# Issuing the first image pair's four lines alternately from SyncE and ScalarE, with the projection weight moved behind them

## The chip, the cores and the metric

One core of a Trainium2 chip runs the program. The metric is the device time of one execution in microseconds; most executions of one kernel here fall within about 2 us of each other (0.2%). The kernel before takes 1033.91 us (median), so two per cent, the threshold for "faster" or "slower", is 20.7 us.

## The reference, cut to what matters

```python
# q: 4 x 12288 x 128, kv: 4 x 384 x 32 x 128, w_sr: 128 x 128, all float32
kv_pool = kv.reshape(B, H // 4, 4, W // 4, 4, C).mean(axis=(2, 4))
k = v = kv_pool.reshape(B, -1, C) @ w_sr          # 768 keys a batch
a = softmax(q @ k.T / sqrt(C)); x = a @ v          # attention
out = (relu(x @ w_gate) * (x @ w_val)) @ w_out     # gated feed-forward, d_ff 1536
```

The keys need 4 x 4 pixels of the image averaged and projected by `w_sr`. Nothing can be scored before the first 256 keys exist.

## The kernel before

The image of a batch is loaded in three "pairs" (of key chunks); each pair is four "lines" (`dh` = 0 to 3) of 128 x 1024 floats, 512 KB a line. In the opening (batch 0) TensorE sums the pixels by accumulating transposes in PSUM: eight transposes a line. Then come a copy, the projection by `w_sr`, the scores, the exponentials and the values. Eight filler matmuls ahead of it are to bring TensorE to its full rate.

```python
    def kv_load(b, pair):
        parts = work.tile([128, r, 2, r, C], FP32, tag="kv_in", bufs=3)
        rows = kv[b, ...].rearrange("(hp dh) (wp h dw) c -> dh hp wp (h dw c)", ...)
        for dh in range(r):                       # one DMA a line, all from SyncE
            nc.sync.dma_start(parts[:, dh].rearrange("p h dw c -> p (h dw c)"), rows[dh])
    ...
    w_sr_f32 = const.tile([128, C], FP32)
    nc.scalar.dma_start(w_sr_f32, w_sr)
    kv_load(0, 0)
    for i in range(0, GRP, 2):
        q_load_plain(i, i + 2)                    # two loads of q, SyncE
    for pair in range(1, NJC // 2):
        kv_load(0, pair)                          # eight more lines, SyncE
    ...
    fill(8)
    ...
    for dh in range(3):                           # TensorE takes the lines in order
        for h in range(2):
            turn_add(h, line(0, dh, h), first=dh == 0)
    for h in range(2):
        turn_end(h, line(0, 3, h), (nc.vector, nc.scalar)[h])
    for h in range(2):
        project_chunk(h, (nc.vector, nc.scalar)[h])
    ...                                           # q casts, scores, exponentials, values
    # GpSimd waits for line 2 of the third pair, then loads the feed-forward weights
    nc.gpsimd.tensor_copy(gate, line(2, 2)[:, 0, 0, 0:1])
```

From about 31 us on a long body of fixed order runs, bound by TensorE.

The softmax here doesn't subtract the row's maximum and nothing guards it: scores larger than these inputs give would overflow.

## Time and profile before

| | kernel before |
|---|---|
| median time | 1033.91 us |
| span of the profiled execution | 1031.3 us |
| TensorE's share of the chain that ended last | 98% |
| landing of the four lines | 5.2, 6.5, 8.5, 9.75 us |
| projection of the first pair starts | 10.83 us |
| body starts (first feed-forward matmul) | 30.30 us |

How to read it: a shift of a few tenths of a microsecond in the opening can't be seen in shares of a 1031 us span. It is read from the time at which the same instruction starts in two traces. I use two such marks, the start of the first projection and the start of the body. Landing times here are the last of the 16 completions that a transfer leaves in the trace. I take each completion for that of one of the core's 16 DMA engines; the trace doesn't name the engine. The single completions come from the trace's own list, which no view prints.

### The profile page before, as it was taken

Reading aid. Unit: us, or ns where it says so; the run is one execution under the profiler, and the core shown is the slowest. Engines: PE = TensorE matmul, PEld = TensorE weight load, DVE = VectorE, ACT = ScalarE, POOL = GpSimd, SP = SyncE. Lnnn points to the kernel's source line nnn. Section 1 sums busy time; section 2 is a strip of 40 time slices with the busy share of each in tenths; the row PEclk is TensorE's granted clock in tenths of the full one; section 3 lists DMA queues with packets and bytes.
Section 4 is the critical chain, followed back from the end, with each engine's and each line's share of the span. In section 5 each row is a group of like instructions: output and inputs, shape, how many; then the busy total and the mean of one; then the engine's idle time right before and its main releaser. Section 6 shows DMA issues by size and latency. Waiting matters only on the chain.

```text
span 1031.3 us, 20032 instructions
## 1 busy us (share of the span) xinstructions
PE 1024.4 (99%) x6580; PEld 546.0 (53%) x6580; DVE 910.0 (88%) x1671; ACT 908.8 (88%) x1745; POOL 279.4 (27%) x287
## 2 busy tenths in 40 slices
PE   8999999999999999999999999999999999999998
PEld 6555555555555555555555555555555555555555
DVE  3889899998989898998889898989888898989898
ACT  4988888889888889888888898888888988888987
POOL 2212146521211125642212121664121221111110
PEclk9999999999999999999999999999999999999999
DMA  8836396462542547836345157573652434513222
GB/s 305 122 57 76 90 195 144 79 93 42 82 69 48 80 120 162 169 53 90 52 68 86 33 84 151 131 173 57 85 73 46 73 54 65 87 32 65 34 40 54
DMA packets 328824, 93.34 MB, mean 91 GB/s; under 512 B 308496, under 2 KB 321936, under 8 KB 328720
## 3 DMA queue, kind: packets, MB, share of 16 engines
q1 hardware_dynamic: 313488, 78.69, 38.7%
q0 software_dynamic: 14944, 13.24, 10.9%
q8 instruction: 51, 0.84, 0.4%
q14 instruction: 53, 0.43, 0.1%
q10 hardware_dynamic: 288, 0.13, 0.0%
HBM read 53.94 MB, written 26.35 MB: 78 GB/s over the span
## 4 chain that ended last, share of the span: by engine, by line
PE 98%; ACT 1%; DMA 1%; SPq 0%; DVE 0%; issue 0%; ACTq 0%
PE bank_ps L279 24%; PE bank_ps L290 24%; PE bank_ps L314 23%; PE bank_ps L241 13%; PE bank_ps L230 12%; PE bank_ps L300 1%; DMA parts<-in_kv_dram 1%; PE bank_ps L163 1%; ACT aT L231 0%; PE bank_ps L189 0%; PE bank_ps L181 0%; SPq L139 0%; ACT val L283 0%; ACT kv L183 0%; PE bank_ps L119 0%
## 5 line engine op out<-in xcount | busy, mean ns | idle before, releaser
L293 DVE SCALAR_TENSOR_TENSOR hT<-bank_ps,val 128x512 f16<-128x512 f32 x1152 | 757.9, 686 | 91.1 <-ACT val L283 70.5
L283 ACT CAST val<-bank_ps 128x512 f16<-128x512 f32 x1152 | 677.8, 589 | 102.5 <-PE bank_ps L279 100.5
L279 PE MATMUL bank_ps<-xT,wv 128*128 128x512 f16 x1152 | 436.6, 379 | 0.2 <-DVE rinv L249 0.2
L290 PE MATMUL bank_ps<-xT,wg 128*128 128x512 f16 x1152 | 436.6, 379 | 0.0
L314 PE MATMUL bank_ps<-hT,wo 128*128 128x512 f16 x1116 | 423.0, 379 | 0.0
L231 ACT ACTIVATE aT<-bank_ps 128x512 f16<-128x512 f32 x576 | 345.8, 604 | 1.0 <-PE bank_ps L230 1.0
L324 POOL TENSOR_SCALAR o_sb<-o_t 128x512 f32<-128x512 f32 x93 | 138.3, 1487 | 694.1 <-DVE rinv L249 660.0
L241 PEld LDWEIGHTS <-aT 128*128 128x128 f16 x2304 | 177.3, 98 | 133.1 <-issue 0.9
L241 PE MATMUL bank_ps<-kv,aT 128*128 128x129 f16 x2304 | 223.6, 220 | 0.0
L230 PE MATMUL bank_ps<-qT,kv 128*128 128x512 f16 x576 | 217.3, 379 | 0.4 <-DVE qT L122 0.2
L279 PEld LDWEIGHTS <-wv 128*128 128x128 f16 x1152 | 112.7, 98 | 132.7 <-issue 0.3
L290 PEld LDWEIGHTS <-wg 128*128 128x128 f16 x1152 | 112.7, 98 | 67.3
L314 PEld LDWEIGHTS <-wo 128*128 128x128 f16 x1116 | 109.2, 98 | 65.9 <-issue 0.2
L230 PEld LDWEIGHTS <-kv 128*128 128x128 f16 x576 | 56.1, 98 | 67.6 <-issue 0.8
L257 DVE TENSOR_TENSOR x<-bank_ps,rinv 128x256 f16<-128x256 f32 x190 | 80.6, 424 | 6.6
L322 DVE STREAM_TRANSPOSE o_t<-bank_ps 128x512 f32<-128x512 f32 x93 | 65.7, 706 | 0.0
L86 POOL DMA_DIRECT2D q<-in_q_dram x88 | 48.3, 556 | 0.3 <-issue 0.3
L148 POOL TENSOR_TENSOR s<-parts 128x512 f32<-128x512 f32 x36 | 44.8, 1265 | 0.0
L249 DVE RECIPROCAL rinv<-bank_ps 128x2 f32<-128x2 f32 x192 | 27.9, 146 | 0.8 <-PE bank_ps L241 0.8
L150 POOL TENSOR_TENSOR s<-s 128x512 f32<-128x512 f32 x18 | 22.8, 1266 | 1.4
L152 POOL TENSOR_TENSOR c<-s 128x256 f32<-128x256 f32 x18 | 13.0, 724 | 1.4
L300 PEld LDWEIGHTS <-hT 128*128 128x128 f16 x144 | 10.1, 98 | 5.8
(53 smaller groups left out, 94.6 us busy)
## 6 DMA issues: line engine op xcount, KB each, us to landing
parts<-in_kv_dram SPq DMA_DIRECT2D x48, 512.0 KB, 6.5
out_dram<-o_sb SPq DMA_DIRECT2D x353, 64.0 KB, 2.2
q<-in_q_dram POOLq DMA_DIRECT2D x88, 128.0 KB, 4.6
xT<-x SPq DMA_TRANSPOSE x94, 2.4
out_dram<-o_sb SPq DMA_DIRECT2D x80, 16.0 KB, 1.5
placed<-blocks SPq DMA_DIRECT2D x9, 128.0 KB, 1.8
kvT<-placed SPq DMA_DIRECT2D x36, 32.0 KB, 1.9
q<-in_q_dram SPq DMA_DIRECT2D x2, 512.0 KB, 8.0
```

The costliest lines, as they stand in the source:

```text
L86: nc.gpsimd.dma_start(q16[32 * j : 32 * (j + 1)].rearrange("t (i s) c -> t i s c", i=GRP), rows[j])
L230: nc.tensor.matmul(s_ps, kv16[:, k // NST, jc, 0:C], qT_of(k), start=True, stop=True)
L231: nc.scalar.activation(aTs[k][:, jc, :], s_ps, AF.Exp, scale=qk_scale)
L241: nc.tensor.matmul(x_ps[:, i, :], aTs[k][:, jc, s * 128 : (s + 1) * 128], kv16[:, k // NST, jc, C : 2 * C + 1], start=(jc == 0 and i == 0) ...
L257: nc.vector.tensor_tensor(x16s[k][:, 2 * half : 2 * half + 2, :], x_ps[:, :, 0:C], rinv.to_broadcast([128, 2, C]), op=ALU.mult,)
L279: nc.tensor.matmul(va_ps, wv16[:, fb * 128 : (fb + 1) * 128], xTs[k], start=True, stop=True)
L283: nc.scalar.copy(val, va_ps)
L290: nc.tensor.matmul(g_ps, wg16[:, fb * 128 : (fb + 1) * 128], xTs[k], start=True, stop=True)
L293: nc.vector.scalar_tensor_tensor(hTs[k][:, fb, :], g_ps, 0.0, vals.pop((k, fb)), op0=ALU.max, op1=ALU.mult)
L314: nc.tensor.matmul(o_banks[k], wo16[:, fb, :], hTs[k][:, fb, :], start=fb == 0, stop=fb == NFB - 1)
L322: nc.vector.transpose(o_t, o_banks.pop(k))
L324: nc.gpsimd.tensor_scalar(o_sb.rearrange("t j s c -> t s j c"), o_t.rearrange("t (s j c) -> t s j c", s=NS, j=4), 1.0 / X_SCALE**2, None, ...
```

## The change

Its intent is to get the first pair's lines in sooner, by having two engines issue them side by side, and to let the weight, which isn't needed until the projection, go after them.

```diff
-    def kv_load(b, pair):
+    def kv_load(b, pair, queues=(nc.sync,)):
...
-            nc.sync.dma_start(parts[:, dh].rearrange("p h dw c -> p (h dw c)"), rows[dh])
+            queues[dh % len(queues)].dma_start(
+                parts[:, dh].rearrange("p h dw c -> p (h dw c)"), rows[dh]
+            )
...
-    nc.scalar.dma_start(w_sr_f32, w_sr)
-    kv_load(0, 0)
+    kv_load(0, 0, (nc.sync, nc.scalar))
+    nc.sync.dma_start(w_sr_f32, w_sr)
```

The values and scores in TensorE's waits of the opening, which the change's name also mentions, stand in both kernels alike.

## The prediction

> **What bounds the kernel now.** I read the page first, then the chain of waits, the timeline of the opening, the transfers, and the landings.
>
> The page's busy shares and chain give the scale:
>
> ```profile
> span 1031.3 us, 20032 instructions
> PE 1024.4 (99%) x6580; PEld 546.0 (53%) x6580; DVE 910.0 (88%) x1671; ACT 908.8 (88%) x1745; POOL 279.4 (27%) x287
> ...
> PE 98%; ACT 1%; DMA 1%; SPq 0%; DVE 0%; issue 0%; ACTq 0%
> ```
>
> TensorE is 98% of the chain that ended last; the change touches nothing in the body after about 31 us, where its order of work is fixed. So the change can only shift the body earlier or later by whatever the opening gains or loses. The chain of waits in the first 12 us shows the part in question:
>
> ```profile
> 0.73 0.70 SPq L139
> ...
> 2.10 0.60 SPq L139
> 2.71 0.04 issue
> 2.75 7.00 DMA parts<-in_kv_dram
> 9.75 0.04 issue
> 9.79 1.09 PE bank_ps L163 x8
> 10.88 0.86 PE bank_ps L181 x4
> ```
>
> SyncE issues the four lines of the first image pair one after the other (about 0.65 us each). The fourth lands at 2.75 + 7.00 = 9.75 us, and TensorE then needs only its own eight transposes, 1.09 us, before the projection. Read naively, three SyncE issues (0.70, 0.58, 0.60, with gaps 2.0 us) stand on the path and an alternation would save most of half of them. The transfers' rate, by slices of 1 us over the first 40, and TensorE's timeline say otherwise:
>
> ```profile
> GB/s 0 50 142 274 397 377 381 434 414 418 410 418 414 418 410 397 414 418 410 397 377 49 10 111 167 195 155 123 110 145 187 188 179 132 143 222 181 130 1 16
> ...
> 5.23 3.13 PE L163 MATMUL bank_ps<-ident,parts 128*128 128x128 f32 x16
> 8.53 1.09 PE L163 MATMUL bank_ps<-ident,parts 128*128 128x128 f32 x8 [0.17 <-DMA parts<-in_kv_dram]
> 9.79 1.09 PE L163 MATMUL bank_ps<-ident,parts 128*128 128x128 f32 x8 [0.17 <-DMA parts<-in_kv_dram]
> ```
>
> From 4 us to 21 us the transfers run at about 410 GB/s without a gap: a 512 KB line every 1.28 us, while SyncE issues one every 0.65 us. Single issues taken by narrow windows land 4.5, 5.0, 6.4 and 7.0 us after issue, that is at 5.2, 6.5, 8.5 and 9.75 us. So the waiting time of line four is the queue, not its issue. What is lost is the ramp: 142 and 274 GB/s in the third and fourth microseconds.
>
> The durations by tile in narrow windows show a second fact:
>
> ```profile
> L163 PE MATMUL bank_ps<-ident,parts x10: 421/421/476, 5.2 to 7.2; 128*128 128x128 f32 x10
> L163 PE MATMUL bank_ps<-ident,parts x8: 273/273/328, 9.8 to 10.6; 128*128 128x128 f32 x8
> ```
>
> The same transpose takes 421 ns (start to start 213 ns) up to about 7.5 us and 273 ns (start to start 109 ns) afterwards. TensorE is slow until then, although the eight filler matmuls began at 1.71 us and the transposes follow them with no pause. The arrival of lines one by one hides this: the 16 slow transposes of lines one and two are done before line three is there.
>
> **What the Trainium skill says.** "DMA: Bandwidth & Descriptors", section "Issuing engines are not separate DMA queues": transfers started by SyncE, ScalarE or GpSimd run on the same 16 engines and interleave; issuing from several saves only issue time. The trace agrees that issue time is not the limit (0.65 us of issue against 1.28 us of transfer). The same page, "Queues, rings and completion order": each DMA engine takes turns, packet by packet, between the queues that have work. Nothing in this trace has two full hardware queues at once, so it isn't shown yet. "TensorE: Matmul & The Clock Gate", Part 1: the array runs at half rate until an activity window of about 3.4 us, free-running, was busy. The trace agrees with the halving (213 against 109 ns), and the switch came at about 7.5 us, 5.8 us after the fillers began, so one mostly busy window did not do.
>
> **The change, part by part.** The work on every compute engine is the same in number and order; only four issues and the weight's load move.
>
> 1. *Issue.* Lines one and three stay with SyncE, two and four go to ScalarE, w_sr goes to SyncE as its third transfer. All four lines are issued by about 2.1 us instead of 3.35. ScalarE's two issues end there, its table load (1.28 us) and warm-up follow, done by about 3.7 us; its first real work is at 10.92 us. Cost on the path: 0. Gain on the path: 0, as the queue is the limit.
>
> 2. *Transfer of the sum.* Four lines are 2 MB whichever queue. w_sr (64 KB) moved at about 2 us, in the empty ramp; now it goes behind line three in a full queue: 64/512 of 1.28 us = 0.16 us later for what comes after it. Two queues from the start may shorten the ramp. About 0.7 MB is missing in it: (410-142)+(410-274) KB = 0.4 MB in two slices and the rest before, so at most 0.4/0.41 = 1 us is there to be had; I allow 0.3 us (choice). Net: the fourth line lands at about 9.75 - 0.3 + 0.16 = 9.6 us, range 9.0 to 9.9.
>
> 3. *Order of landing.* If the engines take turns, lines one and two share the rate and land together, at about 6.4 us (where line two landed), and three and four together, at about 9.5 us. TensorE takes the lines in order. Line one now comes 1.2 us later and line three 1 us later than before.
>    - *TensorE already at full rate:* 16 transposes remain after 9.5 us: 16 x 0.109 = 1.75 us, to 11.25, where before the last eight ended (by start of the projection, 10.83). Loss 0.4 us. Break-even is a landing at 9.1 us.
>    - *TensorE still slow:* fillers end at 5.31; it idles until 6.4. If the window from about 4.2 to 7.6 (the one that seems to have switched it before) isn't busy enough, the switch comes one window later, near 11. Then lines one and two take 16 x 0.213 = 3.4 us, to 9.8; six more by 11.06; ten at 0.109: 12.15. Loss 1.3 us.
>
> 4. *After that.* From 9.79 us to 31 us the chain is compute (transposes, projection, exponentials), so a loss passes whole to the end. A gain passes only as far as the later pairs' lines allow: by their landing times (issue plus time to landing in narrow windows: 5.14 + 9.7, 5.97 + 10.2 and 6.62 + 10.8, so 14.9, 16.2 and 17.4 us for the second pair's last three) TensorE or VectorE takes them up within 0.15 to 0.4 us, so beyond 0.4 us only what the whole stream gains counts.
>
> Sum: probability 0.45 of +1.3 (slow), 0.35 of +0.4 (fast, together), 0.2 of -0.5 (better ramp). 0.585 + 0.14 - 0.1 = +0.6 us. 1033.9 + 0.6 = **1034.5 us**.
>
> **Rivals.**
> - *Issue was the limit:* the fourth line comes 1.3 us sooner (3.35 to 2.1) and the time falls to about 1032.7. For it: the chain names SyncE for 2 us. Against: 10 us of queue before each later landing, and an unbroken 410 GB/s.
> - *The ramp doubles with two queues:* the stream moves up 0.5 to 0.9 us, all pairs with it, and the time is about 1033.2. For it: packets in the ramp move at a third to two thirds of the rate while the DMA engines show over 80% busy (0.89 and 0.83 in these two slices), so each is waiting on something that a second queue might overlap. Against: the engines may be as slow for both.
> - *Hidden anyway:* losses and gains cancel, 1033.9. For it: before, TensorE idled only 0.2 and 0.2 us by the waits view for lines three and four; but the idle time of the pipelined transposes understates it.
> - *w_sr late:* it would hold the projection. Against: it is ahead of q in SyncE's queue and needed a microsecond after line four. No cost.
>
> **Range and chances.** The outcomes span -1.2 (issue theory) to +1.8 (slow, late landing). I take 1033.2 to 1035.8 for 8 in 10. Two per cent is 20.7 us, longer than the whole stretch to which the change reaches, so "within 2%" is 0.99.
>
> **What the profile after would show.** Right: lines one and two landing within 0.3 us of each other near 6.4 us, three and four near 9.5; transposes of 421 ns still running after 8 us; the projection starting at 11.2 to 12.2 instead of 10.83; the body after 31 us equal in length. Wrong: line one still at about 5.2 us (no taking of turns); the GB/s of the third and fourth slice above 300 (the ramp was the queue's); a projection before 10.5 us. The prediction fails if two queues fill the ramp, or if TensorE switches to full rate early however long it waits.

## The result

The changed kernel took 1033.65 us (median of 5 runs, 1033.19 to 1034.54) beside 1033.91 us of the kernel before. The ratio is 0.9999 with a 95% interval from 0.9984 to 1.0013: the same. (A ratio is the mean time of one kernel's fast runs over that of the other's of the same rounds, so not quite the ratio of the medians.)

The chain of waits of the changed kernel in the first 12 us, start, duration, what:

```profile
1.48 7.49 DMA parts<-in_kv_dram
8.96 0.04 issue
9.01 1.97 PE bank_ps L165 x16
10.97 0.86 PE bank_ps L183 x4
```

The reader is to see two things against the chain of before. The last line that TensorE needs is there at 8.96 instead of 9.75 us, 0.78 us sooner. And 16 transposes stand behind it where eight stood: 1.97 us for 1.09 us. The gain is given back on the spot, and the projection (L183) starts at 10.92 instead of 10.83 us.

TensorE's timeline in the same stretch (start, duration, group, idle before and its cause):

```profile
6.39 1.97 PE L165 MATMUL bank_ps<-ident,parts 128*128 128x128 f32 x16 [1.24 <-DMA parts<-in_kv_dram]
9.01 1.97 PE L165 MATMUL bank_ps<-ident,parts 128*128 128x128 f32 x16 [0.65 <-DMA parts<-in_kv_dram]
```

The lines are taken in two blocks of two, with a wait before each. The transfers in narrow windows of issue time (queue, size, us from issue to landing; the first two lines were issued at 0.73 us by both engines, the other two at 1.41 and 1.48 us) tell why:

```profile
parts<-in_kv_dram ACTq DMA_DIRECT2D x1, 512.0 KB, 4.3
parts<-in_kv_dram SPq DMA_DIRECT2D x1, 512.0 KB, 5.6
...
parts<-in_kv_dram ACTq DMA_DIRECT2D x1, 512.0 KB, 7.2
parts<-in_kv_dram SPq DMA_DIRECT2D x1, 512.0 KB, 7.5
```

ScalarE's line two landed first, at 5.07 us; SyncE's line one, which TensorE needs first, only at 6.35 us. Lines four and three came nearly together, at 8.60 and 8.96 us. The transfers' rate by slices of 1 us over the first 40 is:

```profile
GB/s 0 0 123 303 418 418 434 394 417 414 414 397 414 418 410 401 410 418 410 406 369 29 62 164 204 189 106 108 169 159 185 187 131 52 146 232 160 131 0 16
```

The ramp is hardly shorter than before (123 and 303 against 142 and 274 GB/s in the third and fourth slice). So the 0.78 us don't come from moving more bytes. They come from the last completion, which I read as the slowest engine's: in the trace of before, the last completion of line four stood 1.38 us after the first one (9.75 and 8.37 us); in the changed kernel, line three's stand 0.72 us apart (8.96 and 8.24 us). This lag doesn't grow afterwards. In the trace of before it is 1.37 to 1.39 us in each of ten loads in a row, from line four to the load that lands at 21.27 us, and in the changed kernel 0.69 to 0.73 us in eleven. So in this stretch no engine falls further behind: the time is lost once, in the first lines, and the later loads land late by it.

From the projection on, the changed trace is the trace of before, later by a constant: +0.09 us at the projection, +0.09 us at the body's start (30.39 us) and at 475 us, +0.15 us at the end, where another 0.07 us arose at 687 us.

### The profile page after: what moved, and what is told of

It is laid out like the page before. It is cut to its first block, busy times and chain, and to the rows that moved or that the text cites. A ratio compares the mean times of both kernels' runs of the same rounds, so it can differ in the third digit from the quotient of the medians.

```text
span 1031.5 us, 20032 instructions
## 1 busy us (share of the span) xinstructions
PE 1023.0 (99%) x6580; PEld 544.8 (53%) x6580; DVE 910.1 (88%) x1671; ACT 909.1 (88%) x1745; POOL 279.9 (27%) x287
## 4 chain that ended last, share of the span: by engine, by line
PE 98%; DMA 1%; ACT 1%; DVE 0%; SPq 0%; issue 0%; ACTq 0%
PE bank_ps L281 24%; PE bank_ps L292 24%; PE bank_ps L316 23%; PE bank_ps L243 13%; PE bank_ps L232 12%; PE bank_ps L302 1%; DMA parts<-in_kv_dram 1%; PE bank_ps L165 1%; ACT aT L233 0%; PE bank_ps L191 0%; PE bank_ps L183 0%; ACT val L285 0%; ACT kv L185 0%; SPq L139 0%; PE bank_ps L119 0%
```

## The experiments

The theory after the result: **(L)** two queues bring the last line 0.6 to 0.8 us sooner, by keeping the 16 DMA engines closer together, but the lines' order and spacing turn this into twice the work after the last landing. The rivals: **(W)** the weight's move, not the queues, brought the line forward; **(R)** TensorE's rate at that time decides the outcome, that is, when its transposes go from 213 to 109 ns apart ("the switch"; that a pause of TensorE before it delays it is what the expectations call the clock theory); **(C)** the trace of one execution is chance.

The edits shown are against the changed kernel; a4's is against the kernel before, c1's against b4 and c4's against c1. All times that decide are read from traces. The timed medians differ by less than the spread of the runs: the kernel before took 1032.65 to 1035.02 us in 26 runs (mean 1033.63) and the changed kernel 1033.17 to 1034.81 us in 10 (mean 1033.91).

### a1_before_again: the kernel before, again

No edit.

> The kernel before, unchanged, as a second look at its opening. If what I read in its first trace is a property of the kernel, the four lines land again near 5.2, 6.5, 8.5 and 9.75 us, the slowest of the 16 DMA engines again 1.4 us behind the fastest, and the projection starts at 10.8 us. If the late slowest engine was chance (rival), the fourth line lands anywhere from 9.0 to 9.8 us and the projection between 10.1 and 10.9 us. The moment at which the transposes go from 213 to 109 ns apart (7.5 us in the first trace) will move by up to 3 us without moving the projection.

Measured: lines at 5.46, 6.74, 8.30 and 9.75 us; slowest engine 1.16 us behind in line four; projection at 10.83 us, body at 30.30 us, span 1031.3 us. Time 1033.21 us (4 runs; ratio to before 0.9995, interval 0.998 to 1.001). TensorE was at full rate from its first transposes this time, 109 ns apart, and the projection didn't move. So with the switch at 7.6 us (first trace) or by 5.5 us (here) the kernel before starts its projection at the same time, as predicted: each line's eight transposes fit into the wait for the next. A switch after 8.5 us was not seen in it, and would not be hidden: eight transposes at 213 ns are 1.7 us, more than the 1.26 us between its last two lines (an estimate from these two traces). For line four, the second trace of the kernel before speaks against rival C.

### a2_after_again: the changed kernel, again

No edit.

> The changed kernel, unchanged, as a second look. Landing theory: ScalarE's line lands first (5.1 us), SyncE's first line 1.3 us after it, lines three and four within 0.4 us of each other near 8.6 to 9.0 us, and the projection starts at about last landing + 1.95 us = 10.9 us. Clock theory: if TensorE is still at half rate at 6.4 us in this run, the projection starts near 12.2 us and the run is about 1.3 us longer; that would also explain the spread of its timed runs (1033.2 to 1034.5).

Measured: lines two, one, four, three at 5.05, 6.31, 8.65 and 8.93 us, as in the first trace. But this time TensorE was slow. Its timeline, and its transposes by tile in the window 6.5 to 8.3 us (duration min/median/max in ns), beside the same row of the first trace of the changed kernel:

```profile
6.35 6.04 PE L165 MATMUL bank_ps<-ident,parts 128*128 128x128 f32 x32 [1.04 <-DMA parts<-in_kv_dram]
12.33 0.90 PE L183 MATMUL bank_ps<-kvT,w_sr_f 128*128 128x128 f32 x4
...
L165 PE MATMUL bank_ps<-ident,parts x9: 417/418/473, 6.3 to 8.1; 128*128 128x128 f32 x9
```

```profile
L165 PE MATMUL bank_ps<-ident,parts x16: 272/273/327, 6.4 to 8.1; 128*128 128x128 f32 x16
```

All 32 transposes run in one piece of 6.04 us without a further wait: 213 ns apart up to 11.2 us, 109 ns after. The landings no longer matter. The projection starts at 12.33 us, the body at 31.80 us: +1.50 us at both. The span is 1033.0 us (another 0.2 us was lost at 687 us), the time 1034.28 us (4 runs, 1033.8 to 1034.81; ratio 1.0005, interval 0.999 to 1.002). Rival R is thus real: the same kernel with the same landings has a fast and a slow outcome. What differs from the kernel before is that TensorE idles from 5.3 to 6.35 us. But the two fast traces of the changed kernel idle there too (from 5.16 to 6.39 us, and from 5.31 to 6.38 us in c3), and their transposes run 109 ns apart from the first on. So the pause alone doesn't make the slow outcome, and what does is not shown.

### a3_wsr_only: only the weight's move

```diff
-    kv_load(0, 0, (nc.sync, nc.scalar))
+    kv_load(0, 0)
     nc.sync.dma_start(w_sr_f32, w_sr)
```

> Part alone: all four lines stay with SyncE, only the weight w_sr moves behind them. If the earlier fourth line of the changed kernel (8.97 instead of 9.75 us) comes from two queues, this one lands at 9.7 us or later and the projection starts at 10.8 us or later. If it comes from taking the weight out of the start of the stream (rival), it lands near 9.0 us and, as the lines come one by one, the projection starts near 10.1 us, 0.7 us before both kernels.

Measured: lines at 4.76, 6.03, 8.71 and 10.00 us, projection at 11.09 us, body +0.33 us, span 1031.6 us; time 1033.72 us (ratio 1.0, interval 0.9985 to 1.0015). TensorE's timeline:

```profile
8.75 1.09 PE L165 MATMUL bank_ps<-ident,parts 128*128 128x128 f32 x8 [1.32 <-DMA parts<-in_kv_dram]
10.04 1.09 PE L165 MATMUL bank_ps<-ident,parts 128*128 128x128 f32 x8 [0.20 <-DMA parts<-in_kv_dram]
```

The four lines come one by one, and late. The weight's move alone gains nothing; rival W falls. Here the engines were 0.4 us apart in the first two lines and 1.8 and 1.6 us apart in the next two: at least one engine fell behind at the third line.

### a4_alt_only: only the two queues

```diff
     nc.scalar.dma_start(w_sr_f32, w_sr)
-    kv_load(0, 0)
+    kv_load(0, 0, (nc.sync, nc.scalar))
```

> Part alone: the weight stays ScalarE's first issue, then lines two and four go to ScalarE. Two-queue theory: the four lines land by 9.0 us as in the changed kernel, with lines three and four together, projection at about last landing + 1.95 us = 10.9 us. Since ScalarE issues the weight first (0.38 us), I expect SyncE's line to be first in landing order here (5.2 us) and ScalarE's second. Weight theory: the fourth line at 9.7 us and the projection at 11.6 us.

Measured: lines one to four at 5.05, 6.34, 8.74 and 9.21 us, the first two in TensorE's order, as expected. Projection at 10.70 us, body at 30.16 us (-0.14 us); span 1031.4 us, as 0.17 us were lost at 182 us. Time 1033.13 us (ratio 0.9993, interval 0.9976 to 1.001). The two queues bring the fourth line forward by 0.54 us without the weight's move, and again one block of 16 transposes follows:

```profile
8.78 1.97 PE L163 MATMUL bank_ps<-ident,parts 128*128 128x128 f32 x16 [1.09 <-DMA parts<-in_kv_dram]
```

In the changed kernel it was 0.78 us. Whether the weight's move, beside two queues, is worth the other 0.25 us, one trace can't tell: the last landing varies from 8.81 to 9.08 us among the other traces with two queues.

### b1_swapped: the two queues exchanged

```diff
-    kv_load(0, 0, (nc.sync, nc.scalar))
+    kv_load(0, 0, (nc.scalar, nc.sync))
```

> The changed kernel with the two queues exchanged: lines one and three from ScalarE, two and four from SyncE; TensorE still takes the lines in order. In both traces of the changed kernel ScalarE's line landed first (5.05 to 5.07 us) and SyncE's 1.3 us after it, so TensorE waited for the later one. Landing theory: line one now lands at 5.1, two at 6.35, three at 8.6, four at 8.95 us; TensorE starts at 5.1 instead of 6.4 us, is kept busy after the fillers, is at full rate by 8.5 us[...], and the projection starts at 10.5 to 10.6 us (8.65 + 16 x 0.109 + 0.2) in every run: about 1033.2 us, without runs of the 1034.5 kind. Rival, that the first queue to land is chance or is SyncE's when asked first: no change from the changed kernel (10.9 or 12.3 us).

Measured: lines one to four at 4.97, 6.22, 8.47 and 8.85 us; projection at 10.43 us (-0.40), and the body at 30.15 us (-0.15): 0.25 us of it was lost at 23.46 us, where TensorE waited for the last line of the third pair, landed at 23.33 us. Time 1032.93 us in six runs, 1032.66 to 1033.08, the narrowest spread of all; ratio 0.9992, interval 0.9978 to 1.0005, so not shown faster by the times. The landing theory holds: the four landings came within 0.13 us of the expected ones, and the projection 0.07 us before the expected 10.5 us:

```profile
5.10 2.26 PE L165 MATMUL bank_ps<-ident,parts 128*128 128x128 f32 x16
8.51 1.97 PE L165 MATMUL bank_ps<-ident,parts 128*128 128x128 f32 x16 [1.16 <-DMA parts<-in_kv_dram]
```

ScalarE's first line lands before SyncE's here as well. In every trace in which both engines issued a line at 0.73 us, ScalarE's issue ended first (1.36 to 1.39 us against 1.42 to 1.44 us) and its line landed first. In a4, where ScalarE issued the weight first, SyncE's line had its issue ended first (1.42 us against 1.77 us) and landed first. So the queue whose issue ends first lands first in all ten two-queue traces; that the end of the issue is the cause is my reading.

### b2_after_fill11: no pause for TensorE

```diff
-    fill(8)
+    fill(11)
```

> The changed kernel with 11 filler matmuls for 8, so that TensorE is busy from 1.7 us to the landing of line one near 6.35 us (11 x 0.427 + 1.71 = 6.41). Clock theory: TensorE is then at full rate by 8.5 us[...], the projection starts at 10.9 to 11.1 us in every run, and the slow outcome (12.3 us) is gone; median near 1033.5 us. Rival, that the slow second trace came of something else than the pause: the spread of the runs stays as it was, 1033.2 to 1034.8 us.

Measured: the switch came at 7.6 us, projection at 11.03 us (last landing 9.08 + 1.95), body +0.20 us. Four runs of 1033.05 to 1033.74 us (median 1033.24; ratio 0.9996, interval 0.9981 to 1.0011). No slow outcome was seen. Four runs are few, so this agrees with the clock theory and doesn't prove that the pause was the cause.

### b3_after_fill0: no fillers

```diff
-    fill(8)
```

> The changed kernel without fillers: TensorE's first work is at about 6.35 us. Clock theory: [...]the switch comes between 9.8 and 13.2 us and the projection starts between 11.6 and 13.4 us; time 0.7 to 2.5 us above the changed kernel's fast runs, so 1034 to 1035.5 us. Rival, that the rate has no share in it: projection at 10.9 us, time unchanged.

Measured: 213 ns apart from 6.29 to 9.3 us, then 109 ns; projection at 11.35 us, body +0.52 us, time 1034.13 us (4 runs, 1033.64 to 1034.9; ratio 1.0004, interval 0.9989 to 1.0019).

```profile
6.29 5.11 PE L165 MATMUL bank_ps<-ident,parts 128*128 128x128 f32 x32 [6.29 <-DMA parts<-in_kv_dram]
11.35 0.90 PE L183 MATMUL bank_ps<-kvT,w_sr_f 128*128 128x128 f32 x4
```

The sign is as the clock theory has it. The size is less: the switch came 3.0 us after the first transpose, at 9.3 us and not at 9.8 us or later, and the projection 0.25 us before the earliest that I had allowed. TensorE had done nothing but transposes until then, so here transposes alone brought it to the full rate. This one execution without fillers had its projection 1 us earlier than the slow execution of a2, which had eight: in a2 the fillers bought nothing, in the two other traces of the changed kernel 0.4 us.

### b4_first_on_act: line one alone on ScalarE

```diff
-    kv_load(0, 0, (nc.sync, nc.scalar))
+    kv_load(0, 0, (nc.scalar, nc.sync, nc.sync, nc.sync))
```

> Only line one goes to ScalarE, lines two to four to SyncE, the weight after them. Landing theory (two full queues make lines three and four land together): here they come one after the other, at about 7.7 and 8.95 us, only eight transposes remain after the last, and the projection starts near 10.1 us, 0.7 us before both kernels; time near 1032.9 us. Rival (a single queue lets one DMA engine fall behind from its third line on, as in all three traces with the four lines on SyncE, where the fourth landed at 9.75 to 10.0 us): line four at 9.6 to 10 us and the projection at 10.7 to 11.1 us, no gain.

Measured: lines at 4.99, 6.26, 7.55 and 8.89 us, one by one; the engines 0.65 to 0.67 us apart in each. TensorE's timeline:

```profile
5.10 1.04 PE L165 MATMUL bank_ps<-ident,parts 128*128 128x128 f32 x8
...
7.60 1.09 PE L165 MATMUL bank_ps<-ident,parts 128*128 128x128 f32 x8 [0.20 <-DMA parts<-in_kv_dram]
8.93 1.09 PE L165 MATMUL bank_ps<-ident,parts 128*128 128x128 f32 x8 [0.24 <-DMA parts<-in_kv_dram]
9.97 0.90 PE L183 MATMUL bank_ps<-kvT,w_sr_f 128*128 128x128 f32 x4
```

With the early fourth line *and* single spacing the projection starts at 9.97 us, 0.86 us before the kernel before. This is theory L shown from its other side: keep the early landing, take away the doubling, and the gain appears. But it doesn't reach the end:

```profile
23.26 1.07 PE L165 MATMUL bank_ps<-ident,parts 128*128 128x128 f32 x8 [0.29 <-DMA parts<-in_kv_dram]
```

At 23.26 us TensorE waits for the third pair's last line (landed at 23.13 us; in the kernel before at 23.09 us, when TensorE came to it at 23.63 us). Of 0.86 us, 0.34 us are left at the body's start (29.95 us), and these were lost at 685 us, at a later batch's projection, whose operand landed at 685.05 us. Span 1031.3 us, time 1033.18 us (5 runs; ratio 0.9996, interval 0.9981 to 1.0011).

### c1_first_act_proj11: the same, with the later projections a step later

```diff
-                    if odd and step == 10:
+                    if odd and step == 11:
                         project(b, pair)
```

> The kernel with line one alone on ScalarE, and the later batches' projection one step (1.3 us) later in TensorE's order. In that kernel's trace the head gained 0.86 us, 0.34 us of it was left at 30 us, and that too was lost at 685 us, where TensorE waited for a projection's operand that came from the transfer queue. Theory: with the projection a step later the operand is there, the 0.35 us stay, and the time is 1032.7 to 1032.9 us. It also repeats the head: line four again by 9.0 us and the projection of the opening near 10.0 us, or, if the even landing of the 16 engines was chance, near 10.8 us. Rival for the loss at 685 us: another wait follows at once and the end does not move.

Measured (the four c runs, and the runs of the kernel before beside them, ran on chip 11; the a and b runs on chip 4): the head, that is the opening up to the first projection, repeated (lines at 5.15, 6.41, 7.68, 9.03 us; projection at 10.11 us, -0.72 us). This time already the third line of the third pair was late (22.13 us), and all of the gain was gone at 23.2 us. The operand of the projection at 685 us was there (683.3 us), but 0.17 us were lost right behind it, at 687 us: the rival's "another wait follows at once". Span 1031.5 us, time 1033.25 us (5 runs, 1032.64 to 1034.12; ratio 0.9997, interval 0.9984 to 1.0009). The expected 1032.7 to 1032.9 us was missed; the end did not move.

### c2_wsr_only_again: one queue, again

No edit against a3.

> Second look at the four lines on SyncE with the weight behind them. Theory (one queue lets one DMA engine fall behind): the slowest engine is 1.2 us or more behind the fastest in line four, which lands at 9.6 to 10.0 us. Rival (chance): it lands at 8.8 to 9.2 us with the engines 0.7 us apart, as in the two-queue kernels.

Measured: lines at 4.99, 6.37, 8.35 and 9.68 us, engines 1.37 us apart in line four, 0.67 us in line one. The slowest engine again fell behind at the third line. Projection at 10.76 us, but the third pair's last line landed at 24.15 us and the body started 0.92 us late; 1034.09 us, a single run of unknown state.

### c3_after_third: the changed kernel, a third time

No edit.

> Third look at the changed kernel[...]: lines land as in the two traces (5.05, 6.3, 8.6 and 8.95 us for lines two, one, four and three) and the projection starts at 10.9 us if the transposes run 109 ns apart from the start, at up to 12.4 us if they run 213 ns apart until 11.3 us; whatever the rate, start of the projection and start of the body (30.4 to 31.8 us) shift by the same amount.

Measured: lines two, one, four, three at 5.08, 6.34, 8.59 and 8.96 us; transposes 109 ns apart from the first on; projection at 10.92 us, body +0.08 us, 1033.17 us (one run, state unknown). The fast outcome of the first trace, to 0.01 us.

### c4_first_act_gate: the weights' loads a line later

```diff
-    nc.gpsimd.tensor_copy(gate, line(2, 2)[:, 0, 0, 0:1])
+    nc.gpsimd.tensor_copy(gate, line(2, 3)[:, 0, 0, 0:1])
```

(on top of c1)

> As the first of this call, and GpSimd's weight loads wait for the last line of the third pair instead of the last but one. In the kernels with an early head that last line landed at 23.1 to 23.3 us, 1.9 us after the fastest engine's part, while the weights' loads had been issued since 20.7 us, and TensorE lost 0.25 to 0.48 us there. If the weights' loads slow it, it now lands by 22.0 us and the head's whole 0.8 us reaches 30 us (time 1032.3 to 1032.6). Rival: the weights and the second query group come 1 us later, hold TensorE between 30 and 40 us, and the time is the same or worse.

Measured: the third pair's last line landed at 23.45 us all the same, with the weights not yet issued, so they aren't what slows it. The rival came true: q's second group and its transpose were late. The chain of waits from 30 to 42 us:

```profile
27.69 7.86 DMA q<-in_q_dram
...
35.70 5.31 DMA qT<-q
41.01 0.05 issue
41.06 0.39 PE bank_ps L232
```

TensorE stood still for 1.9 us before the score at 41.06 us. Time 1034.35 us (5 runs, 1033.33 to 1035.54; ratio 1.0006, interval 0.9992 to 1.002).

### The traces side by side

| kernel | lines' queue | last line's landing | work behind it | projection | body |
|---|---|---|---|---|---|
| before (2 traces) | SyncE | 9.75, 9.75 | 8 | 10.83, 10.83 | 30.30, 30.30 |
| a3, c2 | SyncE, weight behind | 10.00, 9.68 | 8 | 11.09, 10.76 | 30.63, 31.22 |
| changed (3 traces) | both in turn | 8.96, 8.93, 8.96 | 16 (a2: rate-bound) | 10.92, 12.33, 10.92 | 30.39, 31.80, 30.38 |
| a4 | both, weight first | 9.21 | 16 | 10.70 | 30.16 |
| b1 | both, exchanged | 8.85 | 16 at 8.47 | 10.43 | 30.15 |
| b4, c1 | ScalarE one, SyncE three | 8.89, 9.03 | 8 | 9.97, 10.11 | 29.95, 30.29 |

The four traces with all lines on one queue have the last one at 9.68 to 10.00 us, the ten with two queues (b2, b3 and c4 are the three not in the table) at 8.81 to 9.21 us. The 16 completions of that last line lie 1.2 to 1.6 us apart in the four and 0.5 to 0.9 us apart in the ten. So the effect of issuing from two engines is shown, and chance (C) is out. *Why* a single queue lets a DMA engine fall behind is not: the trace's packets don't name their engine, and no run separated possible causes. One rival stands untested: with two engines every line but the first is also issued sooner, the last by 2.3 to 3.0 us instead of 3.35 us. The last landing doesn't follow that time (b4's last line was issued by 2.94 us and the changed kernel's by 2.29 us, and they landed at 8.89 and 8.96 us), but no run issued the lines sooner on one queue. Nor do all four traces lag alike: before, a3 and c2 lose the time at the third line, while in a1 the completions are 1.2 us apart from line one on. Nor is it settled why the first two lines came whole one after the other while lines three and four overlapped.

b1 has the lowest median, 0.78 us under the kernel before on the same chip (1032.93 and 1033.71 us; seven of the eight runs behind the latter are from the first call), and is the version that I would keep, for its order of landing. Its interval includes 1, so I don't call it faster.

## Why the prediction was right or wrong

The time, 1033.65 us, lies in the range and "within 2%" was right; the centre of 1034.5 us was 0.85 us too high. The hit says little about the mechanism. The range is 2.6 us wide, and the runs of the kernel before alone spread over 2.4 us. The median even moved the other way (-0.26 us) than the first trace (+0.15 us). In the fast branch the loss was 0.09 us and not 0.4 us: the last line came 0.54 us before the 9.5 us that the branch assumed, and its formula left out some 0.2 us. Of the prediction's signs of being right, lines one and two did not land within 0.3 us of each other, lines three and four came together but at 8.60 and 8.96 us and not near 9.5 us, and the projection at 10.92, 12.33 and 10.92 us lay outside 11.2 to 12.2 us each time. Of its signs of being wrong, the fourth slice did pass 300 GB/s (303, with 123 in the third), and TensorE was at full rate in spite of the wait in two of three traces.

- **What bounds the kernel:** right. The opening's shift passed whole to the body: +0.09 us at the projection gives +0.09 us at 30 us, +1.50 gives +1.50, +0.52 gives +0.52. The exceptions are later lines that came late: +0.26 us became +0.33 us in a3, and -0.07 us became +0.92 us in c2, where the third pair's last line landed at 24.15 us. So the stretch up to 31 us is not compute alone, as step 4 has it.
- **Step 1, issue costs nothing:** right for ScalarE's work; its table load ended at 3.34 us and the warm-up at 3.56 us. The four lines were issued by 2.29 us, not 2.1 us. The weight landed at 9.15 us and held nothing.
- **Step 2, landing of the last line:** the mis-sized term. I allowed 0.3 us for the ramp and charged 0.16 us for the weight, 9.6 us in sum, range 9.0 to 9.9. It measured 8.93 to 8.96 us, just under that range. The ramp wasn't the source. The 0.78 us came from the last completions, those of the slowest DMA engine by my reading, which the prediction didn't look at: it read medians to landing and the byte rate, not the spread of the 16 completions.
- **Step 3, order of landing:** half right. Lines one and two did not share the rate: ScalarE's came whole, 1.28 us before SyncE's. Line one still came at 6.35 us, the number predicted, for another reason: by luck. Lines three and four did come together (0.3 to 0.4 us apart), and the stated consequence held: 16 transposes behind the last landing. The break-even was mis-sized: at 8.96 us the projection was 0.09 us late, so it lies at 8.87 us and not at 9.1 us; the formula left out the slower first transpose and the start, some 0.2 us. The sum also starts from 9.5 us, where step 2 ends at 9.6 us.
- **The slow branch, 0.45 at +1.3 us:** it exists. One of three traces of the changed kernel shows it, at +1.50 us with the switch at 11.2 us; there all 32 transposes run without a wait, as the branch has it. That this explains the timed runs' spread is not shown: the kernel before, which shows no such loss in either of its traces, spreads as widely. The prediction's "16 slow transposes of lines one and two" is overstated: in the trace of before, eleven were slow and five already fast.
- **Step 4, a gain passes only in part:** right. Of b4's 0.86 us, 0.34 us reached the body; of b1's 0.40 us, 0.15 us.
- **Rivals:** "issue was the limit" forecast a fourth line 1.3 us sooner and 1032.7 us; the last line came 0.78 us sooner and the time was 1033.65 us. That the earlier issue has a part in the 0.78 us is not excluded (see above). "The ramp doubles" falls with 123 and 303 GB/s beside 142 and 274 before. "Hidden anyway" describes the outcome best, as a cancellation: 0.78 us sooner, 0.88 us more work behind it. "w_sr late" was rightly dismissed: the projection did not wait for the weight.

## What to carry to other kernels

When loads are the limit, look at the order and spacing in which they land and at what work stands behind the last one, not only at their issue: two loads that land together leave twice the work after the end. Give the load that is needed first to the queue that lands first, and look at the spread of the engines' completions, since a load is as late as its last completion. A gain at the start of a long chain must be followed through the next waits before it is counted; here they took more than half of each gain over 0.2 us.

## What the Trainium skill lacked or had wrong

- "DMA: Bandwidth & Descriptors", section "Issuing engines are not separate DMA queues", says that a second issuing engine only saves issue time. The byte rate indeed didn't rise (about 410 GB/s with one queue or two), but the last of four lines landed at 8.81 to 9.21 us with two queues and at 9.68 to 10.00 us with one. As no run separates the second queue from its earlier issue, this doesn't show the sentence wrong. No page mentions that in a burst issued from SyncE alone the last of a load's 16 completions can stand 1.2 to 1.6 us behind its first by the fourth load (0.5 to 0.9 us with two engines issuing).
- The same page, "Queues, rings and completion order", says that an engine takes turns by whole packets of some 9 to 17 descriptors. I read it as an even sharing of two loads. A line is 128 transfers of 4 KB and 16 completions over 16 engines, so nine records an engine if they are shared evenly. If these nine make one packet, which no view shows, the rule has whole lines taking turns, and the first two lines indeed came one after the other, 1.28 us apart. The next two overlapped (8.60 and 8.96 us), which the page's rule doesn't tell. Which queue goes first isn't on the page; in all these traces it was the one whose issue ended first.
- "TensorE: Matmul & The Clock Gate", Part 1, gives a free-running window and about 3.4 us of activity. The runs agree in kind and show how wide the result is: with the same eight fillers from 1.7 us on, the switch came between 5 and 11.2 us, and a pause of 1 us was part of the case that came last. Two other traces with a pause as long came out fast. Without fillers the switch came 3.0 us after the first transpose, with no other work on TensorE.
- No page says how far apart the 16 completions of one load lie when the queues are full: 0.4 to 1.8 us for the first four lines in these traces, and up to 3.0 us for the third pair's.
